# Another order of all steps in a fused attention and channel-mix kernel: batch 0's first token half before its second

## The chip, the cores and the metric

The kernel runs on one core of one Trainium2 chip. The metric is device time in microseconds (us): the median of several runs of the whole program. The kernel before took 189.89 us (three runs, 189.89 to 190.12). The engines are named as in the profile: PE does matrix products, DVE, ACT and POOL work on rows of numbers, SP starts stores, and POOL also starts nearly all loads.

## The reference

For each of 8 batches with 8 heads, 576 tokens and head size 64, keys and values are first pooled into 32 memory slots per head by a softmax of `phi` over the tokens. The queries then attend to these 32 slots. The result, 576 tokens of 512 channels, goes through a channel mix in which each token is blended with the one before it.

```python
a = np.exp(phi - np.max(phi, axis=2, keepdims=True))
a = a / (np.sum(a, axis=2, keepdims=True) + 1e-09)
k_m = np.einsum('bhsm,bhsd->bhmd', a, k)
v_m = np.einsum('bhsm,bhsd->bhmd', a, v)
scores = 1.0 / np.sqrt(q.shape[-1]) * np.matmul(q, k_m.transpose(0, 1, 3, 2))
attn = softmax(scores)                      # 32 slots
x = np.matmul(attn, v_m)                    # to (batch, token, 512)
...
xk = mu_k * x + (1.0 - mu_k) * x_prev       # x_prev: the token before
xr = mu_r * x + (1.0 - mu_r) * x_prev
k = np.maximum(xk @ w_k, 0.0)               # 512 -> 1024
v = k * k @ w_v                             # 1024 -> 512
r = 1.0 / (1.0 + np.exp(-(xr @ w_r)))       # 512 -> 512
out = r * v
```

## The kernel before

All steps are recorded by hand. The table `PLAN` is one long list of words, and the loop at the end of the kernel function goes through it word by word. Each engine executes its own instructions in the order in which the words recorded them, so the table fixes the order on every engine, and the order of the loads on POOL's queue. A word is `who:step`, then `/a` or `/d` for the engine that reads out of PSUM (ACT or DVE), then `@` and the digits of the PSUM banks (0 to 7) that the step takes. A step with a `yield` appears twice or three times: first its matrix products, then what reads them. A bank is taken again only when its reader is done.

Batch 0 is done in another way than the rest. Its steps are `0:exp` (exponential of `phi`), `0:kg` and `0:vg` (pooled keys and values, in halves of the heads), `0:z` (the sums by which they are divided, the denominators of `phi`), `0:h` and `0:tk` (scaled keys, turned), `0:q` (queries turned on DVE), `0:s0` and `0:s1` (scores of token positions 0 to 320 and 320 to 576), `0:es` (their exponentials), `0:l`, `0:r` and `0:y` (denominators as a logarithm, the reciprocal, the weights `atn`). `0:mk` and `0:mr` make the blended inputs `xk` and `xr` in PSUM; the digit 0 stands for the first 256 tokens, 1 for the other 320. `0:uk` and `0:ur` take them out to SBUF as `x0T`. Half 0 needs the weights of positions 0 to 320 alone, half 1 those of both parts. `c0:3b` is key group 3 (128 of the 1024 columns of `w_k`) on the token half b (320 tokens; a is 256). Groups 0 and 1 need the load `p:wk:0-2`, 2 and 3 `p:wk:2-4`, 4 to 7 `p:wk:4-8`. `b:11x6` is eleven products with zeros, 6 times 64 columns wide, which only fill PE's time.

For the batches 1 to 7 the weights of the attention and of the channel mix are multiplied first (`G`, in six projections `Gs0` to `G02`; `E` takes each out of PSUM, `D` forms differences). Then `c1:2` makes a key group straight from the attention weights and `G`: a first product into one bank, a copy of it into another (`/a` or `/d`), and second products with the differences of neighbouring tokens (`d`) into both. `r` is the rectifier, `s` the square. `g` are gates (`r` in the reference), `t` their tanh, `o` the product with `w_v`, which DVE multiplies by the gate and stores. Between scores `1:s` and the weights of batch 1 lie `es` on ACT and, on DVE, `fe`, `fs`, `fo`, `w0`, `w1` and `d`. `1:vm` gives DVE's product of the pooled values with `mu_k` and `mu_r`, which half of the projections read.

Loads go out in the order of the `p:` words. All but `phi` and the keys of batch 0 and the two `mu` go through POOL's queue. The outputs named in `HOLD` (four of batch 0 and one of batch 1) are stored only at the later words `w:`.

Of the kernel before, what the change touches and what calls it, by code (L numbers as in the profile page):

```python
# [16 lines left out]


PLAN = [
# [66 lines left out]
]  # L86

HOLD = ("03", "00", "02", "01", "13",)
# [764 lines left out]
```

## Time and profile before

| | |
|---|---|
| time, median of 3 runs | 189.89 us |
| span of the profiled execution | 187.8 us |
| clock granted to PE | 1.000 over the span |
| DMA read and written | 38.28 MB and 9.44 MB |

The profile gives the span of one execution, from its first to its last instruction; no time of its own is given for that execution beside the span. The median of the runs is 2.09 us above the span: what lies before the first and after the last instruction. Two numbers of one kernel are therefore compared span with span, and 2.09 us are added for a time.

A row of the timeline gives start, length, engine, line, operation, what is written from what, and how many instructions were merged. In brackets stands how long the engine had been idle before it, and what it had waited for. A row of a DMA issue ends with the time from issue to landing. `PEld` is the loading of PE's weights.

### The profile page before, as it was taken

To read this page: it belongs to the slowest core of one execution; us is meant where nothing else is said; L and a number is where in the kernel's file an instruction comes from. 1 tells how busy PE (TensorE), PEld (TensorE's weight loads), DVE (VectorE), ACT (ScalarE), POOL (GpSimd) and SP (SyncE) were. 2 spreads that over 40 slices of the span, in tenths; PEclk is the share of its full clock that TensorE was granted. 3 is DMA by queue.
4 is the path that set the end of the run, shared out by engine and by line. 5 is a ranking of instruction groups with operands and counts; after the bars stand their busy time and mean duration, and the time that the engine had idled before them with its cause. 6 is when DMAs were issued, how large, how long until landed. Compare 5 with 4: busy or idle time off the path is not lost.

```text
span 187.8 us, 6010 instructions
## 1 busy us (share of the span) xinstructions
PE 181.2 (96%) x2483; PEld 103.2 (55%) x2483; DVE 153.9 (82%) x328; ACT 151.9 (81%) x368; POOL 30.2 (16%) x46
## 2 busy tenths in 40 slices
PE   7979999999999999999999999999999999999992
PEld 2544566677644575556544655556545653465441
DVE  2334574899989999999999899999989999889441
ACT  2537889889999999999999889958999678775900
POOL 5943531060303040140032000000000010000000
PEclk9999999999999999999999999999999999999999
DMA  5999999999999999899989995114202224242054
GB/s 188 280 203 220 251 207 205 266 208 234 308 208 210 275 292 255 160 220 224 223 163 237 234 278 197 28 59 113 56 0 59 58 59 113 56 108 63 0 139 140
DMA packets 24923, 31.91 MB, mean 170 GB/s; under 512 B 1880, under 2 KB 19040, under 8 KB 24896
## 3 DMA queue, kind: packets, MB, share of 16 engines
q0 software_dynamic: 17936, 20.45, 59.0%
q1 hardware_dynamic: 5664, 9.00, 17.2%
q10 hardware_dynamic: 1296, 2.08, 3.3%
q8 instruction: 19, 0.31, 0.7%
q14 instruction: 8, 0.07, 0.1%
HBM read 38.28 MB, written 9.44 MB: 254 GB/s over the span
## 4 chain that ended last, share of the span: by engine, by line
PE 90%; DMA 4%; DVE 2%; issue 1%; ACT 1%; POOL 0%; POOLq 0%; DVEq 0%
PE pv L760 34%; PE pk L617 8%; PE pk L625 8%; PE pb L625 7%; PE gps L492 6%; PE pk L599 4%; DMA q<-in_q_dram 4%; PE pr L687 3%; PE pb L687 3%; PE pr L679 3%; PE kvps L312 3%; PE pr L709 2%; PE pr L666 2%; PE scps L395 2%; PE idle L259 1%
## 5 line engine op out<-in xcount | busy, mean ns | idle before, releaser
L760 PE MATMUL pv<-wv,sq 128*128 128x512 bf16 (+3 forms) x296 | 60.5, 350 | 0.0
L760 PEld LDWEIGHTS <-sq 128*128 128x128 bf16 x296 | 27.7, 98 | 24.9 <-issue 2.8
L498 ACT CAST G<-gps 128x512 bf16<-128x512 f32 x67 | 36.2, 629 | 1.2 <-PE gps L492 1.2
L771 DVE SCALAR_TENSOR_TENSOR o<-sg,pv 128x512 f32<-128x512 f32 (+3 forms) x41 | 24.9, 613 | 7.5 <-PE pv L760 5.1
L625 PEld LDWEIGHTS <-G 128*128 128x128 bf16 x224 | 21.4, 98 | 8.5 <-issue 0.7
L583 ACT ACTIVATE rl<-pk 128x288 bf16<-128x288 f32 (+2 forms) x49 | 20.0, 420 | 4.5 <-PE pk L625 3.9
L625 PE MATMUL pk<-diff,G 128*128 128x288 bf16 x112 | 22.9, 286 | 0.0
L625 PE MATMUL pb<-diff,G 128*128 128x288 bf16 x112 | 22.9, 286 | 0.0
L617 PE MATMUL pk<-atn,G 128*128 128x288 bf16 x112 | 20.8, 287 | 0.0
L621 ACT COPY pb<-pk 128x288 f32<-128x288 f32 x41 | 16.4, 410 | 5.1 <-PE pk L617 3.5
L591 DVE TENSOR_TENSOR sq<-rl 128x576 bf16<-128x576 bf16 (+2 forms) x46 | 18.3, 420 | 1.0 <-ACT rl L583 0.5
L583 ACT ACTIVATE rl<-pb 128x288 bf16<-128x288 f32 x40 | 16.2, 427 | 2.2 <-PE pb L625 1.8
L589 ACT ACTIVATE sq<-rl 128x576 bf16<-128x576 bf16 (+2 forms) x26 | 15.7, 624 | 0.5 <-DVE rl L585 0.4
L501 DVE TENSOR_TENSOR G<-G 128x1024 bf16<-128x1024 bf16 x21 | 14.3, 679 | 1.3 <-ACT G L498 1.3
L458 DVE TENSOR_TENSOR atn<-e,lz 128x576 bf16<-128x576 bf16 (+2 forms) x18 | 12.1, 683 | 3.5 <-ACT lz L430 3.5
L617 PEld LDWEIGHTS <-G 128*128 128x128 bf16 x112 | 10.2, 98 | 6.6 <-issue 1.5
L656 ACT ACTIVATE sg<-pr 128x512 f32<-128x512 f32 x22 | 13.0, 618 | 0.7 <-PE pr L687 0.6
L259 PE MATMUL idle<-zeros 128*128 128x512 bf16 (+3 forms) x47 | 12.2, 408 | 1.0 <-DVE zeros L187 1.0
L381 DVE STREAM_TRANSPOSE qT<-q 128x576 uint32<-128x576 uint32 (+2 forms) x16 | 12.1, 765 | 1.2 <-DMA q<-in_q_dram 1.2
L585 DVE TENSOR_SCALAR rl<-pk 128x288 bf16<-128x288 f32 (+2 forms) x23 | 10.1, 449 | 2.8 <-PE pk L599 2.6
L498 DVE CAST G<-gps 128x512 bf16<-128x512 f32 x17 | 11.3, 679 | 0.2 <-PE gps L492 0.2
L292 ACT ACTIVATE em<-ph 128x1152 bf16<-128x1152 f32 (+1 forms) x9 | 9.9, 1095 | 1.6 <-DMA ph<-in_phi_dram 1.6
(101 smaller groups left out, 283.7 us busy)
## 6 DMA issues: line engine op xcount, KB each, us to landing
out_dram<-o SPq DMA_DIRECT2D x46, 128.0 KB, 2.4
ph<-in_phi_dram POOLq DMA_DIRECT2D x7, 576.0 KB, 12.2
q<-in_q_dram POOLq DMA_DIRECT2D x7, 576.0 KB, 13.6
kv<-in_k_dram POOLq DMA_DIRECT2D x7, 576.0 KB, 14.2
kv<-in_v_dram POOLq DMA_DIRECT2D x7, 576.0 KB, 15.0
out_dram<-o SPq DMA_DIRECT2D x6, 256.0 KB, 6.5
out_dram<-o SPq DMA_DIRECT2D x20, 64.0 KB, 2.5
k0f<-in_k_dram ACTq DMA_DIRECT2D x2, 576.0 KB, 5.8
```

The costliest lines, as they stand in the source:

```text
L259: nc.tensor.matmul(ps.rearrange("p (a b) -> p a b", b=64), lhsT=zeros, rhs=zeros[:, :64].unsqueeze(1).to_broadcast([128, blocks, 64]), sta ...
L498: return lambda: copier()(g_tile()[:, v, c, GCOLS[i]], st["gps", v, i][c])
L501: return lambda: nc.vector.tensor_sub(g_tile()[:, 1, :, GCOLS[i]], g_tile()[:, 2, :, GCOLS[i]], g_tile()[:, 0, :, GCOLS[i]])
L583: nc.scalar.activation(rl, ps, AF.Relu, scale=HALF ** 0.5)
L589: nc.scalar.activation(dst, rl, AF.Square)
L591: nc.vector.tensor_mul(dst, rl, rl)
L617: nc.tensor.matmul(pa, lhsT=st["G"][:, 2, c, f], rhs=st["at"][:, c, :NP], start=c == 0, stop=False, skip_group_check=True)
L621: copier()(pb, pa)
L625: nc.tensor.matmul(ps, lhsT=st["G"][:, v, c, f], rhs=st["d"][:, kind, c], start=False, stop=c == 1, skip_group_check=True)
L656: nc.scalar.activation(gated[name], ps, AF.Tanh, scale=0.5)
L760: nc.tensor.matmul(pv[:, cols], lhsT=squares, rhs=wv_sb[:, fi, cols], start=(fi == 0), stop=(fi == NF - 1))
L771: nc.vector.scalar_tensor_tensor(o[:, cols], in0=gated[name][:, cols], scalar=1.0, in1=pv[:, cols], op0=AL.add, op1=AL.mult)
```

## The change

The table `PLAN` is written anew; nothing else in the kernel differs. The functions, the number of matrix products other than the filling ones, all stores' contents and all loads are the same. Both tables hold the same steps, in another order, with other banks and in places another engine for the reading of PSUM. The first lines of the table, before (-) and now (+):

```diff
-    "p:q:0b 0:c01/d 0:exp1 p:v:0h 0:c00/a 0:exp0 b:11x6@5 0:mub@0 0:mub 0:kg0@12 0:c10/d 0:c11/a b:2x8@5 0:kg1",
-    "0:z@0 0:q0 0:z 0:h1/a p:v:0g 0:h0/a b:7x7@5 0:tk@3 0:tk 0:q1 b:2x6@5 0:s0@1204 0:s1@3567 0:es00 0:es10",
...
+    "0:exp0 b:3x8@0 0:mu@3 0:mub@2 0:exp1 0:z@7 0:c00/a 0:c11/a 0:mub 0:mu 0:c01/d b:2x8@1 0:kg0@34 0:c10/d 0:kg1 0:z",
+    "0:h0/d 0:h1/a b:1x8@5 0:tk@5 0:tk p:q:0b 0:q0 p:v:0h 0:q1 b:4x8@6 0:s0@1605 0:es10 0:es00 b:1x8@2 0:s1@0743",
...
```

The filling products go from 47 (21 of 512 columns, the rest narrower) to 29, all of 512 columns.

**DVE at the start, batch 0.** `qT<-q_76` and `q_77` are the turned queries of the two token parts, `rz` the reciprocal denominators of `phi`, `kmT` the turned keys, `atn` the attention weights (320 columns: the first part), `vm` the scaled values, `x0T` the blended input of the channel mix. Before:

```order
L381 STREAM_TRANSPOSE qT<-q_76 128x4x160
L326 RECIPROCAL rz<-zps 128x2
L365 COPY kmT<-ktps 128x256
L381 STREAM_TRANSPOSE qT<-q_77 128x4x128
L458 TENSOR_TENSOR atn<-e,lz 128x320 x2
L458 TENSOR_TENSOR atn<-e,lz 128x256
L521 SCALAR_TENSOR_TENSOR vm<-kvps,rz,mu_m 128x2x64 x2
L458 TENSOR_TENSOR atn<-e,lz 128x256
L545 CAST x0T<-mxps 128x320 x2
```

and now:

```order
L323 RECIPROCAL rz<-zps 128x2
L336 TENSOR_SCALAR kbd<-kvps,rz 128x2x64
L362 COPY kmT<-ktps 128x256
L378 STREAM_TRANSPOSE qT<-q_76 128x4x160
L378 STREAM_TRANSPOSE qT<-q_77 128x4x128
L455 TENSOR_TENSOR atn<-e,lz 128x320
L518 SCALAR_TENSOR_TENSOR vm<-kvps,rz,mu_m 128x2x64 x3
L455 TENSOR_TENSOR atn<-e,lz 128x320
L455 TENSOR_TENSOR atn<-e,lz 128x256 x2
L542 CAST x0T<-mxps 128x256 x2
L542 CAST x0T<-mxps 128x320 x2
```

The reciprocal and the keys no longer stand behind the turning of the first queries, and the token half of 256 columns is taken out of PSUM first.

**POOL's loads after those of batch 0.** `wk`, `wr` and `wv` are the weights, `q_75` and `kv_73` the buffers of batch 1's queries, keys and values. Before:

```order
L208 DMA wk<-in_moe_w_k_dram 128x4x512
L208 DMA wk<-in_moe_w_k_dram 128x4x256 x2
L177 DMA ph<-in_phi_dram 128x4x288
L181 DMA q_75<-in_q_dram 128x4x576
L181 DMA kv_73<-in_k_dram 128x4x576
L208 DMA wr<-in_moe_w_r_dram 128x4x512
L208 DMA wv<-in_moe_w_v_dram 128x8x256
L181 DMA kv_73<-in_v_dram 128x4x576
```

and now:

```order
L205 DMA wk<-in_moe_w_k_dram 128x4x256
L205 DMA wk<-in_moe_w_k_dram 128x4x512
L205 DMA wk<-in_moe_w_k_dram 128x4x256
L174 DMA ph<-in_phi_dram 128x4x288
L178 DMA kv_73<-in_k_dram 128x4x576
L178 DMA q_75<-in_q_dram 128x4x576
L205 DMA wr<-in_moe_w_r_dram 128x4x512
L205 DMA wv<-in_moe_w_v_dram 128x8x256
L178 DMA kv_73<-in_v_dram 128x4x576
```

A quarter of `wk` now comes ahead of its half, and the keys of batch 1 ahead of its queries; up to the values of batch 1 the set of loads is the same in both. Behind them the second half of `wv` now comes ahead of `phi` of batch 2.

**DVE around the weights of batch 1.** `lz` is the spread reciprocal of the denominators, `atn` the weights of batch 1, `diff` their differences, `vM` the values with `mu`, `o` an output of batch 0, `G` the projections. Before:

```order
L447 STREAM_TRANSPOSE lz<-se 128x18x2x32
L473 TENSOR_TENSOR vM<-vtps,mu_116 128x256
L468 COPY vT<-vtps 128x128
L771 SCALAR_TENSOR_TENSOR o<-sg,pv 128x256 x3
L458 TENSOR_TENSOR atn<-e,lz 128x576 x2
L507 TENSOR_TENSOR diff<-atn 128x576
L508 TENSOR_TENSOR diff<-atn 128x2x287
L509 TENSOR_SCALAR diff<-atn 128x2
```

and now:

```order
L444 STREAM_TRANSPOSE lz<-se 128x18x2x32
L455 TENSOR_TENSOR atn<-e,lz 128x576 x2
L504 TENSOR_TENSOR diff<-atn 128x576
L505 TENSOR_TENSOR diff<-atn 128x2x287
L506 TENSOR_SCALAR diff<-atn 128x2
L768 SCALAR_TENSOR_TENSOR o<-sg,pv 128x256
L470 TENSOR_TENSOR vM<-vtps,mu_116 128x256
L768 SCALAR_TENSOR_TENSOR o<-sg,pv 128x256 x3
L495 CAST G<-gps 128x512
```

The weights and their differences now stand ahead of `vM` and of the first outputs, which stood ahead of them.

125 rows, old and new, of the table PLAN are left out of this document.

## The prediction, made before the changed kernel ran

> **What bounds the kernel now.** I read the shares of the engines and of the chain first, then stretches of the span.
>
> ```profile
> PE 181.2 (96%) x2483; PEld 103.2 (55%) x2483; DVE 153.9 (82%) x328; ACT 151.9 (81%) x368; POOL 30.2 (16%) x46
> PE 90%; DMA 4%; DVE 2%; issue 1%; ACT 1%; POOL 0%; POOLq 0%; DVEq 0%
> L259 PE MATMUL idle<-zeros 128*128 128x512 bf16 (+3 forms) x47 | 12.2, 408 | 1.0 <-DVE zeros L187 1.0
> 30.00:35.00 5.00, 5.00 (x79) 2.82 (x67) 2.88 (x7) 4.97 (x16) 0.67 (x1) 1.00 1.23 252
> 35.00:40.00 5.00, 5.00 (x127) 3.43 (x125) 4.91 (x11) 3.75 (x9) 1.22 (x2) 1.00 1.32 219
> 49.40:184.30 134.90, 134.82 (x1686) 74.24 (x1685) 122.92 (x248) 115.14 (x277) 10.99 (x15) 1.00 0.67 147
> ```
>
> PE is busy for 96% of the span and holds 90% of the chain that ended last. In the rows of stretches the columns after the length are PE, PEld, DVE, ACT, POOL, the granted clock, the DMA share and GB/s. From 49.4 to 184.3 PE is busy for 134.82 of 134.90 us, beside 122.92 on DVE and 115.14 on ACT. So a new order can win only where PE does nothing useful, which is the start: 12.2 us of filling products and the waits between them. Later it can hardly win, and loses if it makes PE wait.
>
> **The start, before.**
>
> ```profile
> 3.08 7.02 DMA q<-in_q_dram
> 10.12 0.84 DVE qT L381
> 9.01 0.44 PE L312 MATMUL kvps<-kv,em 64*32 64x64 bf16 x36 [0.17 <-DVE kv L297]
> 12.40 0.53 PE scps L395 x30
> 15.24 0.77 ACT L413 ACTIVATE e<-scps 128x128 bf16<-128x128 f32 x4
> 15.08 0.88 POOL L208 DMA_DIRECT2D wv<-in_moe_w_v_dram  x1 [1.22 <-DMA kv<-in_v_dram]
> 15.02 0.89 DVE L458 TENSOR_TENSOR atn<-e,lz 128x320 bf16<-128x320 bf16 x2 [2.05 <-ACT lz L430]
> 17.68 0.60 DVE L521 SCALAR_TENSOR_TENSOR vm<-kvps,rz,mu_m 128x128 bf16<-128x128 f32 x2
> 18.20 0.42 DVE L458 TENSOR_TENSOR atn<-e,lz 128x256 bf16<-128x256 bf16 x1
> 19.75 3.54 PE L599 MATMUL pk<-x0T,wk 128*128 128x320 bf16 x24 [0.45 <-DVE x0T L545]
> 23.22 0.42 PE L355 MATMUL mxps<-atn,vm 32*64 32x256 bf16 x16
> ```
>
> The first queries land at 10.1. DVE turns them and only then, at 10.96, takes the reciprocal; scaling and turning the keys takes 1.44 more, and the scores start at 12.40, though the keys were pooled at 9.45. The first part's weights are done at 15.91, the second part's at 18.62. The half that is mixed first needs both, so the first key group waits until 19.75.
>
> **The start, now.** The reciprocal stands ahead of the queries. The keys are scaled half on ACT, half on DVE, so from 9.45 I allow 0.9 for what took 1.44: 10.3. DVE turns the queries in 0.84 and the scores start near 11.15, **1.25 us earlier**. Four more exponentials, 0.77, now stand ahead of the logarithms. Between the two weights of the first part stand three scaled values, which wait for the second half of the values; that had landed when POOL went on at 15.08, so pooled by 15.3, three at 0.3 make 16.2, the weight 0.4: 16.6, where it was 15.9. But half 0 needs no more. Its 16 products (0.42) run from there, its unloading ends at 17.9. The second part's weights end at 17.3, and half 1's mixing, which stands ahead of the first key on PE, at 18.2. **The first key starts at 18.2 in place of 19.75, with 0.42 of mixing already behind it: 1.97 us ahead.** If the quarter of `wk` that it reads came late, this would be lost; it is first of `wk` in the queue now.
>
> **Then the loads decide.**
>
> ```profile
> 11.69 0.74 POOL L181 DMA_DIRECT2D kv<-in_k_dram  x1 [0.56 <-DMA q<-in_q_dram]
> kv<-in_k_dram POOLq DMA_DIRECT2D x1, 576.0 KB, 15.1
> 13.12 0.74 POOL L208 DMA_DIRECT2D wr<-in_moe_w_r_dram  x1 [0.69 <-DMA kv<-in_v_dram]
> wr<-in_moe_w_r_dram POOLq DMA_DIRECT2D x1, 512.0 KB, 16.2
> 17.38 0.75 POOL L181 DMA_DIRECT2D kv<-in_v_dram  x1 [1.42 <-DMA wk<-in_moe_w_k_dram]
> kv<-in_v_dram POOLq DMA_DIRECT2D x1, 576.0 KB, 18.1
> 27.36 0.74 POOL L181 DMA_DIRECT2D kv<-in_k_dram  x1 [2.34 <-ACT rl L583]
> kv<-in_k_dram POOLq DMA_DIRECT2D x1, 576.0 KB, 20.7
> 30.09 1.04 PE L666 MATMUL pr<-wr,x0T 128*128 128x512 bf16 x4
> 31.62 0.49 PE L395 MATMUL scps<-qT,kmT 32*32 32x288 bf16 x32
> 35.61 0.75 PE L312 MATMUL kvps<-kv,em 64*32 64x64 bf16 x72
> 36.30 1.05 PE L760 MATMUL pv<-wv,sq 128*128 128x256 bf16 x8
> 37.18 0.22 PE L463 MATMUL vtps<-identity,vb 128*128 128x128 bf16 x1
> 49.39 0.80 PE L312 MATMUL kvps<-kv,em 64*32 64x128 bf16 x72
> ```
>
> Issue plus latency: the keys of batch 1 landed at 26.8, `wr` at 29.3, the values of batch 1 at 35.5, the keys of batch 2 at 48.1. PE took `wr` at 30.09 and the values at 35.61, 0.1 us after they landed. These loads are one stream that is never out of work (DMA share 1.2 to 1.3 in both stretches to 40 us). The set ahead of the values is the same now, so they land at 35.5 again. That is a wall.
>
> PE needed 15.86 us from the first key to the values. Now the same list lacks the 0.42 of mixing and holds one half output more (0.88, from 36.30 to 37.18): 16.32, so from 18.2 to 34.5. Two waits come in. Batch 1's queries land third, at 26.8, in the place that the keys had; DVE gets to them at about 27.3, behind the last blended inputs, turns them and copies the keys in 1.7, so the scores start at 29.0, and PE has 0.5 us without work ahead of them. The third gate waits 0.7 for inputs that ACT takes out behind the exponentials. That is 35.7. **At the values PE is 0.1 us later than before, with one half output more done: 0.8 ahead, of the 1.97.**
>
> From there to the pooled keys of batch 2 PE took 13.78 us. By the products in the two orders the same work stands ahead of those keys in both; less the half output, 12.9 remain: 48.6 in place of 49.39, just behind the load's 48.1.
>
> ```profile
> 33.56 0.78 DVE L435 STREAM_TRANSPOSE eT<-e 128x576 uint32<-128x576 uint32 x1 [0.96 <-ACT e L409]
> 37.48 0.38 DVE L473 TENSOR_TENSOR vM<-vtps,mu 128x256 bf16<-128x256 bf16 x1
> 41.25 0.53 DVE L509 TENSOR_SCALAR diff<-atn 128x2 bf16<-128x2 bf16 x1
> 38.20 0.41 PE L492 MATMUL gps<-wk,vM 64*32 64x512 bf16 x8
> ```
>
> DVE must keep up with that. Its block for the weights of batch 1 ran from 33.56 to about 41.3 with 1.8 us of other work in it, so 5.95 alone. With scores at 29.0 and exponentials to 30.8 it ends at 36.8, one output follows from 37.2 to 37.6, then `vM`, done at 37.95 as before at 37.86. PE wants it at 38.4: 0.4 us of cover.
>
> **The rest** is the same work.
>
> ```profile
> L498 ACT CAST G<-gps 128x512 bf16<-128x512 f32 x67 | 36.2, 629 | 1.2 <-PE gps L492 1.2
> L621 ACT COPY pb<-pk 128x288 f32<-128x288 f32 x41 | 16.4, 410 | 5.1 <-PE pk L617 3.5 <-DVE o L771 0.8 <-ACT G L498 0.4
> ```
>
> Seven casts of `G` go from ACT to DVE (7 by 0.63, 4.4 us) and seven copies the other way (7 by 0.41, 2.9): ACT has 1.5 us less, DVE about that more, and they have 20 and 12 us to spare after 49.4. The held outputs are stored some 20 us earlier, among loads; with a DMA share of 0.67 there this costs nothing, unless it delays a load that PE waits for. SP's queue holds only stores, and POOL still issues each load in 0.75 us and waits there for buffers. At the tail the same outputs follow one another on PE in both orders. What other banks and neighbours cost PE in the later batches no row shows. Bounds: there is 0.08 us to win by the stretch's row; if PE waited 0.45, as ahead of its first key, in half of the seven batches, 1.6 were lost. I take 0.1, near the row.
>
> **Sum.** 187.8 − 0.8 + 0.1 = 187.1 of span. The median stands 2.1 above the span: **189.2**.
>
> **A rule that speaks against it.** The clock is 1.00 in the stretches, but the first products are slow:
>
> ```profile
> 1.40 0.15 PEld L259 LDWEIGHTS <-zeros 128*128 128x128 bf16 x1 [0.28 <-issue]
> 1.83 0.15 PEld L259 LDWEIGHTS <-zeros 128*128 128x128 bf16 x1 [0.28 <-issue]
> 11.74 0.28 PE L361 MATMUL ktps<-identity,kbd 128*128 128x128 bf16 x2 [0.63 <-ACT kbd L337]
> ```
>
> Filling products of 512 columns start 0.43 apart until 5.2 us, later in half of that. 18 of the 47 are gone, so PE pauses longer: by my times at most 0.75 us, ahead of batch 0's second values, against the 0.63 above, which slowed nothing. If the slow rate came back once at the start, it would cost half of such a stretch, 2.1 us. The Trainium skill ("TensorE: Matmul & The Clock Gate", "What's actually happening") has the clock fall to half after an idle window of about 3.4 us. By that rule the pauses are too short and the sum stays; the trace agrees so far as its 0.63 goes.
>
> **The rivals.**
> - *The whole start reaches the end.* If the loads land earlier, all 1.97 stay: 187.9. Against it: the values were taken 0.1 us after they landed. Chance 0.08.
> - *ACT and DVE eat it in batch 1.* DVE is busy 4.91 of 5 us from 35 to 40, and between the values and batch 2 each key's copy and rectifier and eight outputs must come out of banks in time; 0.8 us lost there gives 190.0. Chance 0.18.
> - *Slower: the scores of batch 1 start late.* The block of 5.95 us now stands ahead of `vM` and of the outputs, which hold banks. Past 29.4 every us of delay of the scores delays the projections by one; from 30.6 on the kernel is slower by over 0.2%. At 31.6, as before, it costs 2.2 less 0.8: 191.3. The way in is the load of batch 1's queries, third in place of second. Chance 0.22.
> - *The slow clock returns at the start*: 2.1 less 0.8, 191.2. Chance 0.05.
> - *The half is first but no key starts earlier*, because `wk` lands late: the wall hides most of it, so it lies inside the forecast.
>
> **How the numbers follow.** The forecast, 189.2 with its own range 188.6 to 189.7, has 0.47. A measurement tells 0.2% of 189.89, 0.38 us, from no change. Faster: the forecast but for 0.03, and the first rival, 0.52. Within: that 0.03 and the second rival but for 0.01, 0.20. Slower: that 0.01 and the last two with a price, 0.28. The range takes in the first rival, the 1.6 (190.7) and the third rival up to scores at 31.2: 187.9 to 190.9.
>
> **What would show it.** In the timeline: the first key group at 18.2, batch 1's scores at 29.0, its values pooled at 35.7 behind two half outputs, batch 2's keys pooled at 48.6, and from there to PE's end again 135 us. A first key after 19.5, scores after 30 or a longer last stretch would prove me wrong.

## The result and the profile after

The changed kernel took 192.68 us (median of 4 runs, 191.92 to 192.82), beside 189.89 us for the kernel before in the same session: a ratio of 1.0143, 95% interval 1.012 to 1.0166. It is slower by 1.4%. The forecast was 189.2, with a range that ended at 190.9. The span grew from 187.8 to 190.8 us.

From the page of the changed kernel: shares of the engines, PE's clock in 40 slices, and the queue that brings instructions.

```profile
PE 180.6 (95%) x2465; PEld 102.2 (54%) x2465; DVE 157.7 (83%) x335; ACT 148.6 (78%) x361; POOL 30.1 (16%) x46
PEclk9979999999999999999999999999999999999999
q8 instruction: 19, 0.31, 0.6%
```

Stretches of the changed kernel (PE, PEld, DVE, ACT, POOL, granted clock, DMA share, GB/s):

```profile
9.00:12.40 3.40, 2.95 (x43) 1.26 (x42) 2.00 (x6) 0.37 (x1) 1.49 (x2) 0.50 1.30 205
30.00:35.00 5.00, 4.35 (x54) 2.03 (x54) 3.44 (x8) 3.99 (x12) 1.48 (x2) 1.00 1.32 204
50.60:187.20 136.60, 134.52 (x1686) 74.44 (x1685) 121.26 (x242) 115.78 (x282) 11.01 (x15) 1.00 0.65 148
```

PE now idles in the long stretch too: of the 2.08 us that are missing there, 1.12 are a wait and 0.96 lie behind its last product, which ended at 186.24. And from 9.0 to 12.4 us it ran at half clock, where the kernel before had the full clock from 5.2 us to its end. The list of PE's waits names something new. Its columns: what was waited for, us in total, how often, the longest.

```profile
PE kvps L309 <- issue: 1.3, 2, 0.9
PE scps L392 <- issue: 1.1, 1, 1.1
```

"Issue" means that the engine waited for nothing that the profile shows. The kernel before has no such wait on PE. The timeline of PE in the changed kernel shows the three places, and the milestones of the prediction:

```profile
10.83 1.81 PE L256 MATMUL idle<-zeros 128*128 128x512 bf16 x4
12.56 0.50 PE L392 MATMUL scps<-qT,kmT 32*32 32x160 bf16 x32
15.43 0.24 PE L309 MATMUL kvps<-kv,em 64*32 64x64 bf16 x8
16.54 0.39 PE L309 MATMUL kvps<-kv,em 64*32 64x64 bf16 x28 [0.88 <-issue]
19.84 4.11 PE L596 MATMUL pk<-x0T,wk 128*128 128x256 bf16 x32
...
28.68 0.62 PE L309 MATMUL kvps<-kv,em 64*32 64x64 bf16 x56
29.71 0.25 PE L309 MATMUL kvps<-kv,em 64*32 64x64 bf16 x16 [0.41 <-issue]
31.41 0.49 PE L392 MATMUL scps<-qT,kmT 32*32 32x288 bf16 x32 [0.38 <-DVE kmT L362]
37.34 0.75 PE L309 MATMUL kvps<-kv,em 64*32 64x64 bf16 x72
50.67 0.80 PE L309 MATMUL kvps<-kv,em 64*32 64x128 bf16 x72
103.06 0.46 PE L392 MATMUL scps<-qT,kmT 32*32 32x288 bf16 x26
104.64 0.31 PE L392 MATMUL scps<-qT,kmT 32*32 32x288 bf16 x6 [1.12 <-issue]
```

Three groups of very short products are broken off in their middle: batch 0's second half of values (0.88 us), batch 1's keys (0.41), batch 5's scores (1.12). Together that is 2.41 us; the span grew by 3.0.

The places have something in common. When PE stopped it had begun 445, 957 and 3257 weight loads and products. Its record also has four instructions that only wait for a semaphore between the second place and the third; with these the numbers are 445 plus 256 times 0, 2 and 11. Queue q8 made 19 transfers of 0.31 MB in all, 16 KB each. The record of single transfers (starts in us; the entry is where PE passed the block end 256 instructions earlier) gives:

```
kernel   block ends at   PE enters it   next one's fetch starts   PE at the end   goes on
after         445            9.62              14.30                  15.67        16.54
after         957           23.93              27.35                  29.30        29.71
after        3257           97.94             102.18                 103.52       104.64
before        958           24.00              26.58                  29.69       no wait
```

In the changed kernel PE goes on 2.24, 2.36 and 2.46 us after the fetch starts. The fetch starts 3.4 to 4.7 us after PE entered the block. From entry to going on that makes 6.92, 5.78 and 6.70 us. So the table suggests: a block of 256 instructions that PE gets through in less time than that leaves it without instructions.

### The profile page after: what moved, and what is told of

Its sections match the earlier page's. It is cut to its first block, busy times and chain, and to the rows that moved or that the text cites. A ratio compares the mean times of both kernels' runs of the same rounds, so it can differ in the third digit from the quotient of the medians.

```text
span 190.8 us, 5980 instructions
## 1 busy us (share of the span) xinstructions
PE 180.6 (95%) x2465; PEld 102.2 (54%) x2465; DVE 157.7 (83%) x335; ACT 148.6 (78%) x361; POOL 30.1 (16%) x46
## 3 DMA queue, kind: packets, MB, share of 16 engines
q10 hardware_dynamic: 1296, 2.08, 3.2%
## 4 chain that ended last, share of the span: by engine, by line
PE 91%; DVE 4%; issue 2%; ACT 1%
PE pv L757 33%; PE pk L614 8%; PE pk L622 7%; PE pb L622 7%; PE gps L489 6%; PE idle L256 4%; PE kvps L309 4%; PE pk L596 4%; PE pr L684 3%; PE pr L676 3%; PE pb L684 3%; PE pr L706 2%; PE pr L663 2%; PE scps L392 2%; ACT e L410 1%
## 5 line engine op out<-in xcount | busy, mean ns | idle before, releaser
L495 ACT CAST G<-gps 128x512 bf16<-128x512 f32 x60 | 31.9, 617 | 1.7 <-PE gps L489 1.6
L653 ACT ACTIVATE sg<-pr 128x512 f32<-128x512 f32 x22 | 13.3, 615 | 8.3 <-PE pr L684 4.2
L614 PE MATMUL pk<-atn,G 128*128 128x288 bf16 x112 | 19.2, 287 | 0.0
L618 ACT COPY pb<-pk 128x288 f32<-128x288 f32 x48 | 18.5, 409 | 0.7 <-PE pk L614 0.5
L495 DVE CAST G<-gps 128x512 bf16<-128x512 f32 x24 | 15.7, 682 | 0.5 <-PE gps L489 0.4
L582 DVE TENSOR_SCALAR rl<-pk 128x288 bf16<-128x288 f32 (+2 forms) x24 | 10.8, 455 | 2.4 <-PE pk L622 1.5
L406 ACT ACTIVATE e<-scps 128x288 bf16<-128x288 f32 x28 | 9.3, 421 | 4.2 <-PE scps L392 4.2
L256 PE MATMUL idle<-zeros 128*128 128x512 bf16 x29 | 10.9, 512 | 1.0 <-DVE zeros L184 1.0
```

Source lines behind the costliest of these rows:

```text
L256: nc.tensor.matmul(ps.rearrange("p (a b) -> p a b", b=64), lhsT=zeros, rhs=zeros[:, :64].unsqueeze(1).to_broadcast([128, blocks, 64]), sta ...
L495: return lambda: copier()(g_tile()[:, v, c, GCOLS[i]], st["gps", v, i][c])
L614: nc.tensor.matmul(pa, lhsT=st["G"][:, 2, c, f], rhs=st["at"][:, c, :NP], start=c == 0, stop=False, skip_group_check=True)
L618: copier()(pb, pa)
L653: nc.scalar.activation(gated[name], ps, AF.Tanh, scale=0.5)
```

## The experiments

**Theory A**: that, called A1 where the fetch is said to wait behind data in the DMA queues, and A2 where only the place of the block end is said to count. **Theory B**: the new order itself, its banks, its waits for DVE and ACT and the slow clock. Times are medians, beside the kernel before in the same session (189.4 to 189.7).

**1 to 4: move the block ends.** A loop of small products behind the first filling ones shifts all later instructions of PE by a number that one can choose, and costs 10 ns each:

```diff
+        for i in range(small):
+            g = slice(i % 4 * 32, i % 4 * 32 + 32)
+            nc.tensor.matmul(ps[g, :16], lhsT=zeros[:64, :32], rhs=zeros[:64, :16],
+                             start=True, stop=True, skip_group_check=True)
-WARM = (10, 8)
+WARM = (6, 8, 102)     # e1; 132 in e2; 46 in e3, in the kernel before
...
-b:2x8@1 0:kg0
+b:5x8@1 0:kg0          # e4 alone
```

> The changed kernel with 196 more PE instructions at its very start: 102 small filling products (each a weight load and a product of 16 columns that computes nothing) in place of 4 of the 10 wide ones. Every later instruction of PE stands 196 places later; the order on all engines is the same. Theory A (PE's instructions arrive in blocks of 256 by DMA, and PE runs dry where a block ends inside a group of very short products): the block ends move to other places of the program, so the three idle times of PE that end with 'issue' (0.88 ahead of batch 0's second half of values, 0.41 in batch 1's keys, 1.12 in batch 5's scores) leave those places; the first key starts at 19.0 to 19.3 instead of 19.84, and the time is 190.2 to 191.8, depending on whether new ones appear. Theory B (the new order itself costs the time: its banks and its waits for DVE and ACT, and the clock halved from 9.0 to 12.4 us): the idle times stay where they are and the time stays at 192.3 to 193.0.

> As the run before, but 256 more PE instructions at the start (132 small filling products for 4 wide ones): one whole block, so by theory A the block ends fall on the same places of the program as in the changed kernel. Theory A: idle times that end with 'issue' return at the same three places (kvps x8 and x28, kvps x56 and x16, scps x26 and x6), and the time is 192.2 to 193.2. If it is not the place of the block ends but the small products themselves (more work early, another clock) that helped the run before, this one helps as much. Theory B: 192.3 to 193.0, the same as the run before.

> The kernel before (its old order) with 84 more PE instructions at the start: 46 small filling products for 4 of its 10 wide ones. Its block ends, by theory A, then stand inside its second group of batch 0's scores and at the ends of three groups of pooled keys. Theory A: at least one idle time of PE that ends with 'issue', which the kernel before has nowhere, and 190.3 to 191.5 instead of 189.9. Theory B: no such idle time, and 189.7 to 190.1.

> The changed kernel with five filling products of 512 columns instead of two ahead of batch 0's pooled keys, to keep the clock up. If the clock halved from 9.0 to 12.4 us because PE had too little work in the stretch before it, the record shows 1.0 through the start now, the four fills ahead of the first scores take 0.9 instead of 1.81 us, the scores start near 12.2 instead of 12.56, and the time falls by 0.3 to 0.5 us to 192.2 to 192.4; by theory A the three idle times stay (6 more instructions move the block ends by 6 places only, still inside the same groups). If the clock at the start is the main cause, the time falls by 1 us or more.

e1 took 192.73 us (ratio 1.0139, interval 1.0065 to 1.0212), e2 193.52 (1.019, 1.0117 to 1.0263), e3 192.09 (1.0132, 1.0071 to 1.0193), e4 192.58 (1.014, 1.0066 to 1.0215). PE's rows that ended with a wait for issue, in e1, with the clock there:

```profile
18.19 1.30 PE L256 MATMUL idle<-zeros 128*128 128x512 bf16 x3 [2.10 <-issue]
...
15.00:20.00 5.00, 2.79 (x57) 1.10 (x56) 2.44 (x7) 2.07 (x7) 2.36 (x3) 0.84 1.26 257
```

in e2:

```profile
10.66 0.23 PE L313 MATMUL kvps<-kv,em 64*32 64x64 bf16 x6 [1.33 <-issue]
17.55 0.39 PE L313 MATMUL kvps<-kv,em 64*32 64x64 bf16 x28 [1.22 <-issue]
30.71 0.25 PE L313 MATMUL kvps<-kv,em 64*32 64x64 bf16 x16 [0.41 <-issue]
105.90 0.32 PE L396 MATMUL scps<-qT,kmT 32*32 32x288 bf16 x6 [1.38 <-issue]
```

in e3, the kernel before with its instructions shifted:

```profile
13.73 0.23 PE L399 MATMUL scps<-qT,kmT 32*32 32x128 bf16 x2 [0.92 <-issue]
55.80 0.40 PE L496 MATMUL gps<-wk,vM 64*32 64x512 bf16 x5 [0.50 <-issue]
```

and the first scores and the broken values in e4:

```profile
11.64 0.38 PE L392 MATMUL scps<-qT,kmT 32*32 32x160 bf16 x32 [0.27 <-DVE qT L378]
16.04 0.61 PE L309 MATMUL kvps<-kv,em 64*32 64x64 bf16 x31 [1.42 <-issue]
```

With 196 more instructions the three waits are gone from their places and one of 2.10 us stands elsewhere. With 256 more they return at the same products (28, 16 and 6 are left over, as in the changed kernel), and one more block end falls into batch 0's keys. The old order, shifted by 84, gets such waits as well, and its time is 2.6 us longer; the two waits are 1.4 us of that, the rest I have not traced. Theory B can't do any of this. My times for e1 were too low: the one wait was nearly as long as the three together, and the clock fell to half behind it. Those for e2 and e3 were too low as well, by 0.3 and 0.6 us. e4 held the clock until 16 us and the first scores came 0.92 us earlier, as expected and more; but PE then reached the block end earlier than its instructions, waited 1.42, and the median stayed, though its four runs spread from 191.35 to 193.55. One run of the changed kernel itself points the same way: its mean clock was 0.996, against 0.989 to 0.991 in the other three, and it took 192.75 us all the same.

**5 to 7: is it the loads?**

```diff
+        elif what == "hold":
+            nc.gpsimd.tensor_copy(mark, state[int(part)]["e"][:1, 0, :1])
...
-5:q0 p:q:7 p:phi:7 ... 5:kv@24 p:k:7 p:v:7 ... 5:s@6702 5:es0 5:es1
+5:q0 ... 5:kv@24 ... 5:s@6702 5:es0 p:hold:5 p:q:7 p:phi:7 p:k:7 p:v:7 5:es1
-WARM = (10, 8)         # e6 and e7, with b:5x8@1 as in e4
+WARM = (10, 8, 17)
```

> The changed kernel with the four loads of batch 7 (queries, phi, keys, values), which went out from 95.7 to 100.6 us, held on POOL until the first exponential of batch 5's scores is done (a copy of one number waits for it), and what reads them (exponential of phi, its sums, the turning of the queries) recorded some 15 us later. PE's instructions stand at the same numbers up to 107 us, so the block end stays inside batch 5's scores. Theory A1 (the next block is fetched when PE enters a block, but behind the data that the DMA engines have queued: at 102.18, 4.2 us after PE entered the block, and PE goes on 2.46 us after that): with no loads in flight the fetch starts within 1.5 us of the block's entry, the idle time of 1.12 in batch 5's scores is gone (under 0.3), and the time falls by 0.7 to 1.1 us to 191.6 to 192.0. Theory A2 (only the place of the block end counts, not the loads): the 1.12 stays. Theory B (order of DVE and ACT): it stays as well, and the time is 192.5 to 193.5.

> The changed kernel with 40 more PE instructions at the start (17 small filling products, and three more wide ones ahead of batch 0's pooled keys). By theory A the block ends move 40 places ahead: out of batch 1's keys, where PE lost 0.41, and into the last third of the groups ahead of the other two places. Worked out from the changed kernel's times with a fetch that needs 6.9 us from a block's entry at the start and 5.9 us until 110 us: 1.7 us of idle time in batch 0's first values (0.88 before, though what follows waits in part for other things), none in batch 1's keys, 0.3 in batch 5's scores. Theory A: time 191.0 to 192.2. Theory B: 192.3 to 193.0 as e4.

> Both of the two runs before together. Theory A1: no idle time that ends with 'issue' after 20 us, and 190.5 to 191.8; still behind the kernel before, since the start stays late. Theory B: 192.3 to 193.5.

PE in e5, then in e6, then in e7:

```profile
103.01 0.48 PE L394 MATMUL scps<-qT,kmT 32*32 32x288 bf16 x32
...
119.30 0.38 PE L321 MATMUL zps<-ones,em 128*128 128x2 bf16 x9 [0.93 <-ACT em L291]
```

```profile
15.21 0.24 PE L313 MATMUL kvps<-kv,em 64*32 64x64 bf16 x9 [1.50 <-issue]
```

```profile
16.29 0.24 PE L315 MATMUL kvps<-kv,em 64*32 64x64 bf16 x9 [2.57 <-issue]
```

In e5 PE entered the block at 97.89, as in the changed kernel (97.94), but the fetch now started at 98.71 and not at 102.18, and batch 5's 32 scores ran without a break, though the block end is where it was. The DMA engines were busy for a share of 0.15 from 97.9 to 98.7, and of 1.11 from 97.9 to 102.2 in the changed kernel. That is A1 against A2. The time did not fall (193.12): the sums of batch 7, which I had moved, now waited 0.93 for their exponential, and what follows 0.20 for DVE's reciprocal. e6 lost the two later waits, as expected, and took 191.42 (1.0115, 1.0067 to 1.0163). e7 lost them too, but took 193.17 where I expected 190.5 to 191.8. The sums of batch 7 waited 0.93 as in e5; and though its rows from 10.2 to 13.3 us are those of e6, its fetch started at 13.90 and not 12.79, and PE waited 2.57 instead of 1.50. Loads were in flight in both (a DMA share of 1.3 behind the block's entry). So the length of the wait is not a property of the program alone, and what in the traffic sets it stays open.

**8: take the wait at the start away.**

```diff
-                for j in range(NJ):
+                js = 3 if b == 0 and parts.start == 1 else NJ
+                for j in range(js):
...
-b:2x8@3 0:mk1@3615
+b:2x8x48@3 0:mk1@3615
```

> The changed kernel with batch 0's pooled values summed over 3 of their 9 token groups (24 products are left out in each half, so the values are not the reference's), and 48 small filling products between the two mixing halves, so that all later instructions keep their numbers. The block end that stood inside the second values now stands behind the first mixing. Theory A: the idle time of 0.88 at the start is gone, the scaled values follow at about 15.9 to 16.2 instead of 17.00, and the first key group starts at 19.0 to 19.3 instead of 19.84; the later idle times (0.41 and 1.12) stay, and the time is 191.8 to 192.2. Theory B, or a start that waits for ACT and the slow clock in any case: the first key group stays at 19.6 or later and the time within 0.3 of 192.6.

```profile
18.30 4.12 PE L601 MATMUL pk<-x0T,wk 128*128 128x256 bf16 x32
...
28.48 0.26 PE L314 MATMUL kvps<-kv,em 64*32 64x64 bf16 x16 [0.63 <-issue]
103.70 0.32 PE L397 MATMUL scps<-qT,kmT 32*32 32x288 bf16 x6 [1.41 <-issue]
```

These rows of e8 show the first key at 18.30, earlier than I expected; the clock stayed at 1.00 there, too, which is not the edit's doing, as the instructions up to these values, at 13.3 us, are the changed kernel's. The later waits stayed. The time was 191.71, which is 2.02 us above the kernel before; the two waits are 2.04. (e8 also has less work ahead of the first key: the 48 products that it leaves out.)

**10 and 11: the price of a block, by itself.** (9 follows below.)

```diff
-p:wr:0-4 g:01@2
+p:wr:0-4 b:0x8x512@2 g:01@2          # e10
-g:70 o:73@5 g:71
+g:70 b:0x8x512@5 o:73@5 g:71         # e11
```

> The changed kernel with 512 small filling products (1024 PE instructions, four blocks, each block 1.2 to 1.4 us of work by the 102 products that took 0.98 us) put ahead of batch 0's first gates, at about 32 us, where the loads of batch 1 and 2 are in flight. Theory A1: PE is idle once in each block, and the first two blocks, fetched beside loads, take 5.5 to 7.5 us each from entry to entry. The time grows by 12 to 25 us. Theory B: 5 us of small products without idle time, and the time grows by 5 us.

> The same 1024 small instructions ahead of the last outputs, at about 180 us, where no load is in flight and only outputs are stored. Theory A1: PE is idle once in each block here too, but a block takes only 2.5 to 4 us (the fetch starts at once; PE goes on 2.2 to 2.5 us after its start), 10 to 15 us in all. Theory A2 (the loads do not matter): as long as beside the loads. Theory B: 5 us without idle time.

PE in e10, among loads, then in e11:

```profile
34.87 1.19 PE L261 MATMUL idle<-zeros 64*32 64x16 bf16 x128 [2.87 <-issue]
40.79 1.19 PE L261 MATMUL idle<-zeros 64*32 64x16 bf16 x128 [4.73 <-issue]
```

```profile
181.28 1.20 PE L261 MATMUL idle<-zeros 64*32 64x16 bf16 x128 [2.63 <-issue]
184.73 1.20 PE L261 MATMUL idle<-zeros 64*32 64x16 bf16 x128 [2.26 <-issue]
```

A block of 128 weight loads and 128 products is 1.2 us of work. Among loads one started every 5.92 us (40.79 − 34.87), with nearly nothing in flight every 3.45. The difference is in the start of the fetch: by the record of transfers it came 3.6 to 3.7 us after PE had entered these blocks in e10 and 1.1 us in e11, and PE went on 2.3 to 2.4 us behind it in both. So 5.92 and 3.45 us are what 256 such instructions of PE cost in the one case and the other, though they hold only 1.2 us of work. The whole program took 216.14 and 208.18 us (one run each), 23.5 and 15.5 above the changed kernel; e11 is a little over my 10 to 15. In both the clock was at half during most of the blocks and for 5 us behind them, so not all of this is the price of fetching.

**9 and 12: a version without the waits.** e9 is e6 with less filling. e12 also records half of the pooled values behind the sums of the scores, so that the block end no longer keeps those sums waiting:

```diff
-b:5x8@7 0:mk0@5067 ... b:2x8@3 0:mk1@3615
+b:2x8@7 0:mk0@5067 ... b:1x8@3 0:mk1@3615        # e9 and e12, WARM = (10, 8, 21)
-0:y00 0:vg1@24 0:l01@0 0:l11@3 b:1x8@5 0:vg0
+0:y00 0:l01@0 0:l11@3 b:1x8@5 0:vg1@24 0:vg0     # e12 alone
```

> The run with 40 more instructions (191.42), with two wide filling products instead of five ahead of batch 0's first mixing and one instead of two ahead of the second, and four more small ones at the start, so that all later instructions keep their numbers. There the five ran at half clock from 16.30 to 18.49, though the weights that the mixing needs were done by about 17.7. If the filling products kept the mixing waiting: mixing from 17.7 to 17.9 instead of 18.49, first key group at 19.7 to 19.9 instead of 20.56, time 190.5 to 191.0. If the idle time of 1.50 ahead of them and the engines behind it decide alone: 191.2 to 191.6. It does not beat the kernel before in either case, as the idle time at the start stays.

> The run with 40 more instructions and less filling (190.17), with batch 0's first half of pooled values recorded behind the sums of its second scores and behind a filling product, in place of ahead of them: the products are the same, only their order on PE differs. The idle time of 1.3 us, which stood inside these values and kept the sums (and behind them the logarithms on ACT) waiting until 15.48, now falls behind the sums. Theory A (the start waits for what PE could not do while its next block of instructions was on its way): sums at 13.6 to 14.0 instead of 15.48, the last reciprocal on ACT at about 16.6, the first key group at 19.0 to 19.6 instead of 20.20, and the time 189.0 to 189.7, level with the kernel before (189.4). If the values and the slow clock after the idle time decide and not the sums: first key group at 19.9 or later, 189.9 to 190.4.

e9 took 190.17 us (12 runs, 189.19 to 191.99) beside 189.39: 1.0038, interval 1.0015 to 1.006. Its mixing began at 18.01 and its first key at 20.20, both somewhat later than expected, but the time is below both of my ranges, and the ratio fell from 1.0115 to 1.0038. e12 took 189.41 (11 runs) beside 189.64 for the kernel before: 0.9993, interval 0.9984 to 1.0002. It does not beat the kernel before by what a measurement can tell. Rows of e12 (PE, one of DVE, and one of PE's weight loads):

```profile
13.93 0.38 PE L421 MATMUL zps<-e,sumh 128*128 128x256 bf16 x2 [0.48 <-ACT e L414]
14.45 0.81 PE L313 MATMUL kvps<-kv,em 64*32 64x64 bf16 x72
15.34 0.87 DVE L522 SCALAR_TENSOR_TENSOR vm<-kvps,rz,mu_m 128x128 bf16<-128x128 f32 x3
18.19 4.11 PE L600 MATMUL pk<-x0T,wk 128*128 128x256 bf16 x32
...
29.23 0.49 PE L396 MATMUL scps<-qT,kmT 32*32 32x288 bf16 x32 [0.38 <-DVE kmT L366]
35.62 0.64 PEld L313 LDWEIGHTS <-em 64*32 64x32 bf16 x72 [0.42 <-DMA kv<-in_v_dram]
35.62 0.75 PE L313 MATMUL kvps<-kv,em 64*32 64x64 bf16 x72
48.77 0.80 PE L313 MATMUL kvps<-kv,em 64*32 64x128 bf16 x72
179.32 3.65 PE L761 MATMUL pv<-wv,sq 128*128 128x512 bf16 x24
```

The values run unbroken, the clock stays up, and none of the three waits of the changed kernel is left. The profiled execution was lucky in one point: its fetch at the start came 3.00 us after the block's entry, where the changed kernel's took 4.68.

## Why the prediction was wrong

**The start at 18.2.** It came at 19.84. The step that failed is "pooled by 15.3" and what follows from it: PE stopped inside the second values for want of instructions (0.88 us), and the scaled values started at 17.00 and not at 15.3. Ahead of that the scores started at 12.56 and not at 11.15, because the half clock stretched four filling products from 1.03 (e4) to 1.81 us and the turning of the keys with them. (With the clock up they start at 11.64 to 11.68, in e4 and e12: 0.5 of my 1.25 us was not there in any case, as the keys were scaled, turned and copied by 10.84 in e4, where I had 10.3.) Where both were gone, in e8 and e12, the first key came at 18.30 and 18.19. In e12 the scaled values ran from 15.34 to 16.21, as I had them. So my chain of DVE, ACT and PE was right; what PE needs beside data was not in it. DVE in the changed kernel:

```profile
17.00 0.87 DVE L518 SCALAR_TENSOR_TENSOR vm<-kvps,rz,mu_m 128x128 bf16<-128x128 f32 x3 [0.79 <-PE kvps L309]
```

**"By that rule the pauses are too short and the sum stays."** The clock did fall, from 9.0 to 12.4 us. In the 3.41 us ahead of that PE's longest wait was 0.51 us, so no single pause decided. The Trainium skill ("TensorE: Matmul & The Clock Gate", "What's actually happening") has a free-running activity window; the trace agrees with its 3.41 us, but a window with few wide products was enough here, without an idle one. The rival of the slow clock had this mechanism, at a chance of 0.05.

**The scores of batch 1 at 29.0, its values at 35.7, batch 2's keys at 48.6.** They came at 31.41, 37.34 and 50.67. e12 has them at 29.23, 35.62 and 48.77, close to the forecast. Its values of batch 1 landed at 35.54 (issued at 16.34, 19.2 us to landing) and PE's weight loads waited for them, so the wall was where I had put it. In the changed kernel they had landed at 34.9, and PE came to them late: its first key was 1.65 us behind e12's, and that carried on, with 0.41 on top of it in batch 1's keys. The rival in which late scores make the kernel slower put the loss behind the scores, in the projections; the loss was already there when they started.

**"The rest is the same work", plus 0.1.** This step failed, too: in the changed kernel it was plus 1.72. A wait of 1.12 us stood in batch 5's scores, and the end of the span came 4.56 us behind PE's last product (190.8 − 186.24) where it had come 3.57 behind it (187.8 − 184.23). No row of before could show the wait. Without it, in e12, PE needs 134.20 us from batch 2's keys to its last product (182.97 − 48.77), where it needed 134.84 (184.23 − 49.39). But from there to the end of the span pass 4.63 us (187.6 − 182.97). The last rows of PE before, then in the changed kernel:

```profile
178.86 1.89 PE L760 MATMUL pv<-wv,rest 128*128 128x512 bf16 x8
180.59 3.64 PE L760 MATMUL pv<-wv,sq 128*128 128x512 bf16 x24
```

```profile
181.61 1.05 PE L706 MATMUL pr<-G,atn 128*32 128x512 bf16 x16
182.59 3.65 PE L757 MATMUL pv<-wv,sq 128*128 128x512 bf16 x24
```

"At the tail the same outputs follow one another" was wrong: a gate now stands ahead of the last 24 products. That the last outputs, finished closer together behind it, are stored later for this reason is argued, not tried. Together it makes +0.42 in e12 in place of +0.1.

**The sum.** The changed kernel's span is 3.7 us above my 187.1: 2.07 at batch 2's keys (50.67 − 48.6) and 1.62 behind them (1.72 − 0.1). The waits for instructions add up to 2.41 us, and the longer end of the span is 0.99; what the slow clock at the start cost by itself is not separated. With the waits gone e12, the new order with other filling products and with its values moved, has 187.6 us of span, where I had 187.1 and the kernel before has 187.8. So the order by itself gains little or nothing that a measurement can tell, and it brought block ends into groups of very short products. No rival of mine had that. It could have been seen: the page of before lists q8 with its 19 transfers, and that order has groups of 144 instructions in 0.75 us. One more term was off, without weight: the median above the span. My 2.1 set the median of some executions against the span of another; in each of the changed kernel's four the time was 1.75 to 1.82 above the span.

## What to carry to other kernels

Where PE runs groups of very short products, count its instructions: 256 of them took 5.92 us beside heavy loads and 3.45 us with nearly none, though they held only 1.2 us of work; in the changed kernel's three places it was 5.8 to 6.9. A new order that shortens the pauses between such groups may gain nothing until the next block has arrived, and adding or dropping a few early instructions moves every later block end. If a wait for issue stands inside a group, test it by shifting the instructions by a part of a block and by a whole one.

## What the hardware showed that I had not expected

PE's instructions arrive in blocks of 16 KB by DMA, one block ahead. While loads were in flight the fetch started some us after PE had entered a block (4.68, 3.42 and 4.24 in the changed kernel's three cases), with the loads held 0.82 after, and 1.1 after where only little was in flight (e11). PE went on 2.2 to 2.5 us after the start in the waits above, once 2.7 (e11). The Trainium skill ("Runtime: NRT & Kernel Launch", "Instruction fetch mechanics") has the 16 KB and a queue of their own, as the traces have, and calls the cost of a block's end mostly hidden; here the waits at block ends were 2.41 us of one kernel, and the measurement decides.

The wait can differ where the instructions ahead of it ran alike: 1.50 us in e6 and 2.57 in e7. e9, with one wait at the start, spread from 189.19 to 191.99 us, the kernel before beside it from 189.15 to 190.15; that the wait makes this spread is not shown, since only one execution was traced, and one of seven runs of the kernel before in another session took 191.40.

The clock changed only at steps of 3.41 us: in the changed kernel at 5.57, 8.98 and 12.40. I weighted each product's columns by the part of the 128 by 128 array that it uses, with 0.216 us for 512 columns on the whole array (8 in 1.73 us in the chain of waits), and took the share of each such window at the start of twelve kernels. The share was 0.22 to 0.30 in all eight windows that half clock followed, and 0.29 or more in all others. This is an estimate from the shapes, not a row, and it moves by some hundredths with the way in which products at the edge of a window are counted; products on a small part of the array keep PE busy in the profile and count for little in it. Where the windows lie is not set by the program: e8 runs the same instructions as the changed kernel until 13.3 us, but its windows began at 4.57 and not 5.57, and its clock stayed at 1.00. So whether the clock falls at the start can differ between executions of one kernel.
